# Transposes of q and x by TensorE in place of transposing transfers, in a linear-attention and MLP kernel

## The chip, the cores and the metric

The kernel runs on one core of one Trainium2 chip. The time is that of one execution on the device in microseconds (us), median of several runs. In the profile the engines are PE (TensorE, matmul) with PEld (its weight loads), DVE (VectorE), ACT (ScalarE), POOL (GpSimd) and SP (SyncE, which here only issues transfers).

## The reference

Eight batches of q, k and v go through linear attention with the feature map elu(x) + 1; the heads are joined to rows of 512, and these go through a two-layer MLP with the tanh form of GELU. Sizes: 8 batches, 8 heads, 576 positions, 64 per head; `w_in` 512 x 2048, `w_out` 2048 x 512.

```python
q_p, k_p = phi(q), phi(k)                       # phi(x) = where(x > 0, x, exp(x) - 1) + 1
kv = einsum('bhsd,bhse->bhde', k_p, v)
z = sum(k_p, axis=2)
num = einsum('bhsd,bhde->bhse', q_p, kv)
den = einsum('bhsd,bhd->bhs', q_p, z)[..., None] + 1e-06
x = (num / den) -> rows of 512 (heads joined), 4608 rows
h = x @ w_in
out = gelu_tanh(h) @ w_out
```

## The kernel before

**Tiling.** A batch has 576 positions. The first 512 are its main part, laid out as four chunks of 128 rows; the last 64 of all eight batches make one more part of 512 rows, the rest. Iterations j = 0 to 8 (`iteration`, L1065) each do the MLP of one part: 0 to 7 the main parts of the batches, 8 the rest. Iteration j also prepares the attention of the next part, and loads and maps for the ones after.

**The MLP of a part.** The hidden layer needs x with its 512 features on the partitions and the 512 rows along the free dimension: `xt`, four feature blocks of 128 x 512. Iterations 0 and 1 form h in sixteen blocks of 128 hidden features (`h_mm`, L354, words `p` in the orders; `g` is the GELU by ACT). From iteration 2 on half, and from 3 on all, of h comes in quads named X, Y, Z and W (`Quad`, L989): a two-by-two product in seven products in place of eight, each of four matmuls with 256 columns. Their operands are sums of quarters of `w_in` and of x; those of x are made by DVE in `sum_x` (L979, word `!xs`), four subtractions from the finished `xt`. Words of a quad are its products (X1 to X7), copies out of PSUM (s, m, u), additions (c, a) and GELUs (g11 to g22). The output layer has the same seven-product form (`Products.seeded`, L860, words `o1` to `o7`, each 16 matmuls with 256 columns; `S1` to `S4` are sums of hidden quarters by DVE, `os`, `ou`, `om`, `oc11` and so on are copies and additions of results).

**The attention of a part.** q, k and v are loaded by SP. The map is three instructions: the exponential by ACT (`!qe`, `!ke`), max(x + 1, 1) by DVE (`!qx`, `!kx`) and the smaller of the two by DVE (`!qm`, `!km`). v is cast by ACT or DVE (`!vc`). `kv_in_pair` (L629, word `k`) forms the key-value sums with 72 matmuls on 64-row tiles. `qt` is the mapped q with the feature dimension on the partitions; `nab` (L313, words `n0` to `n3`) multiplies a chunk of it with the key-value sums into a pair of PSUM banks (`nab_in_banks`, L319, into two single banks), and `divide` (L290) takes reciprocal and product on DVE and writes the chunk of x in rows, `xs`. The rest's q rows come in four tiles (`!rx`, `!re`, `!rm`).

**The transposes before.** In batches 0 and 1 q and x are transposed by TensorE: a matmul with an identity, 128 x 128 at a time into a PSUM tile `t_ps`, and a copy by ACT or DVE (`transpose_q`, L405 and L510; `transpose_x`, L346). For batches 2 to 7 and the rest, SP issues a transposing transfer from SBUF to SBUF for each chunk: `least_q` (L619) issues four for q as soon as the map is done, `least_rest` (L565) one for each rest tile, `transposed_x` (L641), called from `attention_piece` (L648), one for each chunk of x as soon as it is divided. They stand in SP's queue, in program order, between the loads.

**PSUM.** Of eight banks, six are single tiles (tag b): h blocks, quad products, output products, transposed blocks, and pieces in banks. Two form one pair, for attention pieces and key-value sums.

**What sets the order.** Nothing is scheduled at run time: each engine runs its instructions in the order in which the program issues them and waits on semaphores for its operands. That order is written out, one string of words for each iteration (ORDER_A to ORDER_I, L1123 on, for iterations 0 to 8). A prime after a word chooses the other engine for a copy, or for an `n` the two single banks. `@` runs work that is filed under a slot, among it stores; `!t` loads ACT's table for GELU.

Of the kernel before, what the change touches and what calls it, by code (L numbers as in the profile page):

```python
# [10 lines left out]
BF16 = mybir.dt.bfloat16  # L11
# [6 lines left out]
def kernel(  # L18
# [6 lines left out]
    moe_w_out: bass.AP,  # L25
    out: bass.AP,
):

    nc = tc.nc
# [5 lines left out]
    C = 4  # L41
# [40 lines left out]

    def pair_of_banks(name):
        return ps_a.tile([P, 2, 512], FP32, name=name, tag="a")

    ld = {}
# [90 lines left out]
    load_q(3)  # L179

    warm = pg.tile([P, 512], BF16, name="warm", tag="g")
    nc.vector.memset(warm, 0.0)
    ident = pth.tile([P, P], BF16, name="ident")
# [10 lines left out]

    def vp_paired(b):
        return vps[b % 2].rearrange("p (j u) e -> p j u e", u=NP)

    phi, exps, own = {}, {}, {}
# [37 lines left out]
    def least_of(name, b, hs=None, cs=None):  # L240
# [3 lines left out]
        if cs:  # L244
            p, e = p[:, cs], e[:, cs]
        nc.vector.tensor_tensor(p, p, e, op=ALU.min)

    def cast_v_paired(b, us, fn):  # L250
# [138 lines left out]
        nc.scalar.preload_act_table_set("gelu_apprx_tanh_and_others")  # L389

    BEGUN = (0, 1, 2, 3)

    def first_batch():
# [84 lines left out]
    first_batch()  # L480

    FIRST = 2
    fill = {}

# [77 lines left out]

    def least_rest(m):  # L565
        least_of("qr", m)
        if m == 0:
            qts[B] = pt.tile([P, C, NP, P], BF16, name="qt")
        nc.sync.dma_start_transpose(
            out=qts[B][:, m], in_=phi["qr", m][:, 0].rearrange("p h d -> p (h d)")  # L570
        )

    def cast_v_of(b, other):
        fn = nc.vector.tensor_copy if other else nc.scalar.copy
# [43 lines left out]

    def least_q(b, cs=slice(0, C)):  # L619
        least_of("q", b, cs=cs)  # L620
        if b not in qts:
            qts[b] = pt.tile([P, C, NP, P], BF16, name="qt")
        for c in range(cs.start, cs.stop):
            nc.sync.dma_start_transpose(
                out=qts[b][:, c],
                in_=phi["q", b][:, c].rearrange("p h d -> p (h d)"),
            )

    def kv_in_pair(b, fn=nc.vector.tensor_copy):  # L629
        kv_ps = pair_of_banks("kv_ps")  # L630
# [7 lines left out]
                in_=src[r],  # L638
            )

    def transposed_x(b, c, x):  # L641
        if b not in xts:
            xts[b] = pt.tile([P, NP, MAIN], FP16, name="xt")
        nc.sync.dma_start_transpose(out=xt_chunk(b, c), in_=x)

    x_parts = {}

    def attention_piece(b, c, in_banks=False):  # L648

        if b < B:  # L650
            return transposed_x(b, c, (nab_in_banks if in_banks else nab)(qts[b], b, c))
        if b not in x_parts:
            x_parts[b] = pxs.tile([P, C, d_model], FP16, name="xs")
        x = x_parts[b][:, c]
        if in_banks:
            n_ps = [bank("n_ps", [P, 4 * E]) for _ in range(2)]
        else:
            pair = pair_of_banks("n_ps")
            n_ps = [pair[:, s] for s in range(2)]
        bs = 2 * c, 2 * c + 1  # L660
        for i in range(2):
            for a in range(2):
                n = slice(E * (2 * i + a), E * (2 * i + a + 1))
                for t in range(2):
                    r = slice(HP * t, HP * (t + 1))
                    for s in range(2):
                        nc.tensor.matmul(
                            n_ps[s][r, n],
                            lhsT=qts[b][HP * s : HP * (s + 1), c, 2 * a + i, r],
                            rhs=kv_of_head(bs[t], s, 2 * a + i),  # L670
                            skip_group_check=True,
                        )
        x_v = x.rearrange("p (i s a d) -> p s i a d", s=2, a=2, d=D)
        if in_banks:
            for s in range(2):
                divide(x_v[:, s], n_ps[s].rearrange("p (i a e) -> p i a e", a=2, e=E))
        else:
            divide(x_v, pair[:, :, 0 : 4 * E].rearrange("p s (i a e) -> p s i a e", a=2, e=E))
        transposed_x(b, c, x)

    def evac(dst, src, on_scalar):
        (nc.scalar.copy if on_scalar else nc.vector.tensor_copy)(dst, src)
# [22 lines left out]
    def o_mm(o_ps, g, t, ms, half=None):  # L705
        for m in ms:
# [6 lines left out]
                start=(m == 0),  # L713
                stop=(m == MM - 1),
            )

    def w_out_sums():  # L720
# [344 lines left out]
    def iteration(j):  # L1065
# [10 lines left out]
        for word in ORDERS[j].split():  # L1076
# [26 lines left out]
                attention_piece(j + 1, int(name[0]), name.endswith("'"))  # L1103
            elif kind == "k":
                kv_in_pair(int(name))
            elif kind == "S":
                n, ms = name.split(":")
                products.sum(int(n), slice(*map(int, ms.split("-"))))
            elif kind == "T":
                products.third_sum(slice(*map(int, name.split("-"))), False)  # L1110
            elif kind == "!":
                what, _, b = name.rstrip("'").partition(":")
                if what == "vc":
                    cast_v_of(int(b), name.endswith("'"))
                elif b:
                    prepare_of[what](int(b))
                else:
                    prepare[what](j)
            else:
                name, other = name.rstrip("'"), name.endswith("'")  # L1120
                quads[kind].step(int(name) if name.isdigit() else name, other)
# [5 lines left out]
        "@32 o1:12-16 @33 !qe:2 o2:12-16 @34 o3:12-16 @35"  # L1127
    )
    ORDER_B = (
        "p0 !ke:2 p13 !lk:3 p1 !kx:2 !vc:2' !km:2 !t !qx:2 @2 p7 !qm:2 p2 g0 !bq !lv:3 !mq g1 g2 "  # L1130
        "p3 g3 k2 !a0 !a2 !a3 p6 p4 p5 p8 g4 p11 g5 !kxb:3 p9 g6 g7 T0-8 o1 os' g8 g9 p10 !qx:3 "
        "!kxa:3 g10 p12 o7 !lk:4 g11 p14 g12 g13 om S1:0-6 p15 S2:0-5 g14 g15 n1' o2 S1:6-8 "
        "S2:5-8 S4:0-6 n0 oc11' o6 !qe:3 n3' ou S4:6-8 !ke:3 n2 o5 oc22 !lq:4 !km:3 !vc:3 o4 oc21 "
        "o3 oc12' !qm:3 !ke:4 !xs !kx:4"
    )
    ORDER_C = (
        "!br k3 @1 Y1 Z1 !km:4 p6 Zs p0 !lk:5 !t g6 !lv:4 Z2 Zg11 Z6 p14 Z7 p8 Zu Z5 Zm g14 p7 g0 "
        "g8 Ys p15 !qx:4 Zc g7 Y6 Yu' Zg22 Y2 Yg11 Y7 Ym Z4 Za g15 n1 p1 g1 Y5 Yc Zg21 Y4 Ya Z3 "
        "Zg12 S1:4-8 n3 o1 Yg22 S2:4-8 p9 S1:0-1 S2:0-1 n2 Yg21 os g9 Y3 Yg12 S1:1-3 S1:3-4 "
        "S2:1-3 S2:3-4 S3:0-8 !qe:4 n0' o2 !lv:5 !qm:4 o6 oc11 ou o7 om o5 !kx:5 S4:0-8 oc22 "  # L1140
        "!ke:5 !vc:4 !xs o4 oc21 o3 !km:5 k4 oc12"
    )
    ORDER_D = (
        "!lq:5 !w0 Z1 X1 !t Y7 Y1 Xs X2 !w3 X7 @1 Ym' X6 Xg11 Ys n1 Xm' Y2 X4 Y6 Xu Xa X5 Yg11 Zs "
        "Xc Yu Xg21 n0 !lk:6 Y4 !vc:5' Z6 Zu X3 Xg12 Z2 Ya Y5 W1 Z7 Yc Zg11 Ws k5 Xg22 Zm Yg21 W6 "
        "Wu' Z5 Yg22 Y3 Yg12 !lv:6 Zc W7 Wm' W2 Z4 Za W5 Zg22 Z3 Wc W4 Wa n3 Wg11 Zg12 Zg21 o1 "
        "S1:0-6 Wg21 n2 os W3 Wg12 S2:0-6 !lq:6 Wg22 S1:6-8 S2:6-8 o2 !qe:5 S3:0-5 o6 S3:5-8 o7 "
        "S4:0-8 !qx:5 ou !qm:5 om !ke:6 oc11 o5 !lk:7 oc22 !vc:6 !kx:6 o4 o3 oc21 !xs oc12'"
    )
    ORDER_E = (  # L1150
        "X1 X7 Xm Xs Y7 !t X6 X2 Xg11 Xu' @1 Y1 Ym X4 X5 Ys Xa Xg21 Z1 Y2 Yg11 Zs !lr:0 Y4 Xc X3 "
        "!km:6 Y6 Yu n2 Z7 Xg12 Z6 Ya Z2 Zu Xg22 Yg21 n1 Zm W1 Z5 Y5 Yc Zc Zg11 Ws k6 Z4 Yg22 W7 "
        "Za Z3 Wm' Zg22 W6 Wu' n3 W4 Zg12 W2 Wg11 Wa Y3 W5 Wc Yg12 S1:0-6 S2:0-6 Zg21 Wg21 o1 os "
        "n0 Wg22 W3 Wg12 S1:6-8 S2:6-8 S3:0-8 !qx:6 o2 !lv:7 S4:0-8 !qe:6 o6 ou !lq:7 oc11 o7 om "
        "!xs o5 oc22 !re:0 o4 !re:1 !ke:7 !qm:6 oc21 !kx:7 o3 oc12'"
    )
    ORDER_F = (
        "!t !km:7 X1 Y1 Y7 !vc:7' Xs Ym' X6 X7 @1 X2 Xu Y4 Xm' !lr:1 X5 Xc X4 Xa Xg11 Ys k7 Y6 "
        "Yu' Y2 Xg22 Xg21 X3 Z1 Yg11 Zs !qx:7 Y5 W1 Yc Z2 Xg12 Ya Zg11 Z6 Zu Ws' Y3 Z7 Zm n1 Yg12 "
        "Z5 Yg22 W6 Wu S1:0-2 W7 Z4 W2 W5 Wm' Zc !rx:0 Zg22 Z3 Zg12 Wc Wg11 n0 Wg22 W4 S1:2-6 "  # L1160
        "S3:0-6 W3 Wg12 o1 os S1:6-8 S3:6-8 S2:0-8 n3 !qe:7 o7 om' o6 Wa Za Zg21 Yg21 ou' n2 o4 "
        "!qm:7 S4:0-6 o5 oc22 Wg21 o2 !rm:0 oc11 S4:6-8 o3 oc21 oc12 !xs"
    )
    ORDER_G = (
        "X1 n0 !rx:1 !rm:1 Xs Y7 Ym' X7 Xm' X2 X6 Xu' Xg11 Y1 Ys X4 Xa n2 X5 Y2 Z1 Xg21 Y6 Y4 "
        "Yg11 Zs W1 Xc Xg22 Yu' Ya !rx:2 X3 Xg12 Yg21 Y5 @1 Z6 Yc Z2 Z7 Zg11 Zu' Ws' Y3 Z5 Yg22 "
        "W7 Wm' W2 Wg11 Yg12 Zm Zc W6 Wu' W4 Zg22 Wa Z3 Zg12 Z4 W5 Za Zg21 Wc S1:0-6 o1 Wg21 "
        "S2:0-6 os n1 W3 Wg22 Wg12 S1:6-8 S2:6-8 S3:0-8 n3' o2 !rx:3 o6 o7 oc11' !re:2 ou S4:0-8 "
        "om o5 !re:3 !rm:2 oc22 o4 oc21 !rm:3 o3 !xs oc12' !t"
    )  # L1170
    ORDER_H = (
        "X1 Xs X7 Xm' n0' n1 X6 Xu X2 Xg11 X4 Y1 Xa X5 Y7 Xc Ys Y6 Xg21 Y2 Yg11 Yu' Z1 X3 W1 Zs "
        "Y5 Z6 Z2 Xg12 Ym Yc Y4 @1 Z7 Zu' Z5 Xg22 Zg11 Ya Y3 Ws W6 W2 Zm Yg21 Zc W7 Yg22 Wu' Wm "
        "Zg22 Wg11 Z3 Zg12 W5 Z4 Za Yg12 Zg21 Wc Wg22 W4 Wa S1:0-6 o1 os W3 Wg21 S2:0-6 Wg12 "
        "S1:6-8 S2:6-8 S3:0-8 n2 n3' o2 oc11 o6 ou o7 om o5 S4:0-8 o4 oc22 !xs o3 oc21 oc12'"
    )
    ORDER_I = (
        "X1 Y7 Ym X7 Xm Xs X2 Xg11 @1 X6 Y1 X4 Z1 Ys Y6 Xu' Xa Xg21 Y2 Y4 Yg11 Zs X5 Yu' Ya Y5 "
        "Yg21 Z7 Z2 Z6 W1 Xc Xg22 Zg11 Yc Y3 Yg22 Zu' X3 Ws' Z5 W6 Zm Zc Yg12 Wu W2 W7 W5 Wg11 Wm "
        "Zg22 Wc Xg12 Z4 Za Z3 Zg12 W4 Wa W3 Wg12 S1:0-6 S2:0-1 Wg22 o1 S1:6-8 S2:1-8 S3:0-8 o5 "  # L1180
        "Zg21 o6 Wg21 S4:0-8 o7 o2 o4 o3"
    )
    ORDERS = {0: ORDER_A, 1: ORDER_B, 2: ORDER_C, 3: ORDER_D, 4: ORDER_E, 5: ORDER_F, 6: ORDER_G, 7: ORDER_H, 8: ORDER_I}

# [33 lines left out]
```

## Time and profile before

| | |
|---|---|
| median of three runs | 265.94 us (265.37 to 266.69) |
| the profiled execution | 266.18 us |
| its span, first to last instruction | 264.4 us |
| first matmul of iterations 1, 2, 3, 4 | 48.30, 76.27, 104.15, 131.25 us |
| of iterations 5, 6, 7, 8 | 157.66, 184.31, 209.81, 235.33 us |
| end of the last matmul | 260.98 us |
| transposing transfers of x: number, median from issue to landing | 28, 2.3 us |
| of q | 24, 4.1 us |

The page of a profile gives the busy time of each engine over the span, then the span in 40 slices of 6.6 us, with a digit for the busy tenths, the granted clock of TensorE and the busy share of the 16 DMA engines. A view of windows gives the same for chosen stretches of time: length, then busy microseconds and number of instructions of each engine. A view of waits lists which engine sat idle before which tile and line, and what released it. The timeline lists instructions in order: start, duration, engine, line, operation, output and inputs, count. Matmuls overlap in the array, so the duration of a single one is longer than the distance to the next.

### The profile page before, as it was taken

The page shows a single profiled execution, that of the slowest core. Times are in us where ns is not written, and L with a number is a line of the kernel's source. Part 1 is how long each engine was busy: PE and PEld are TensorE (multiplying, and loading weights), DVE is VectorE, ACT ScalarE, POOL GpSimd, SP SyncE. Part 2 cuts the span into 40 slices and gives each one's busy share as a digit, 9 for nine tenths or more (in the row PEclk, how much of TensorE's full clock was granted, in tenths as well). Part 3 has the DMA queues.
Part 4 walks back from the last instruction along what each step waited for, and adds up shares of the span by engine and source line. Part 5 has one row for each costly group of instructions (what it writes and reads, how often), then busy time and mean ns, then how long its engine had stood idle before and what let it go on. Part 6 is the DMA issues. An engine that isn't in the chain of part 4 may idle for free. (4 is left out here: it accounts for less than half of the span.)

```text
span 264.4 us, 6675 instructions
## 1 busy us (share of the span) xinstructions
PE 257.3 (97%) x2765; PEld 203.0 (77%) x2765; DVE 227.7 (86%) x384; ACT 192.1 (73%) x279; POOL 18.8 (7%) x28
## 2 busy tenths in 40 slices
PE   8999999999999999999999999999999999989994
PEld 2584446446876788888888888989889888878883
DVE  3966497799989999999999999999999788868972
ACT  4768795955988788988898988884876478408810
POOL 8056501000000000000000000000000000000000
PEclk9999999999999999999999999999999999999999
DMA  6999999997969969999697398415620450112004
GB/s 235 402 405 397 409 409 396 407 304 217 222 152 286 327 112 222 346 261 241 191 264 195 57 347 236 82 40 68 174 102 21 126 134 2 24 57 121 2 0 159
DMA packets 59789, 53.90 MB, mean 204 GB/s; under 512 B 35696, under 2 KB 45936, under 8 KB 59760
## 3 DMA queue, kind: packets, MB, share of 16 engines
q1 hardware_dynamic: 56880, 44.57, 58.4%
q10 hardware_dynamic: 2880, 8.91, 9.4%
q8 instruction: 21, 0.34, 0.5%
q14 instruction: 8, 0.07, 0.1%
HBM read 36.70 MB, written 9.44 MB: 175 GB/s over the span
## 5 line engine op out<-in xcount | busy, mean ns | idle before, releaser
L784 PEld LDWEIGHTS <-g 128*128 128x128 f16 x624 | 60.5, 98 | 7.8 <-issue 0.4
L784 PE MATMUL o_ps<-w_out_sb,g 128*128 128x256 f16 x384 | 45.7, 273 | 0.0
L356 PE MATMUL h_ps<-xt,w_in_sb 128*128 128x512 f16 (+2 forms) x212 | 37.3, 327 | 0.0
L999 PEld LDWEIGHTS <-w_in_sb 128*128 128x128 f16 x312 | 30.1, 98 | 5.3 <-issue 1.5
L1014 ACT ACTIVATE g<-hq_ps 128x512 f16<-128x512 f32 x52 | 30.9, 622 | 3.9 <-DVE hq_ps L1027 2.5
L356 PEld LDWEIGHTS <-w_in_sb 128*128 128x128 f16 x212 | 18.0, 98 | 14.8
L784 PEld LDWEIGHTS <-s 128*128 128x128 f16 x272 | 26.5, 98 | 3.5
L376 ACT ACTIVATE g<-h_ps 128x512 f16<-128x512 f32 x40 | 22.2, 604 | 8.6 <-PE h_ps L356 8.3
L296 DVE TENSOR_TENSOR xs<-n_ps,r 128x512 f16<-128x512 f32 (+1 forms) x43 | 25.5, 592 | 1.5
L999 PEld LDWEIGHTS <-w_near 128*128 128x128 f16 x224 | 21.6, 98 | 3.5
L999 PE MATMUL hq_ps<-t_sum,w_near 128*128 128x256 f16 x168 | 24.1, 273 | 0.0
L1027 DVE TENSOR_TENSOR rows<-hq_ps,rows 128x512 f32<-128x512 f32 x26 | 17.6, 685 | 1.9 <-PE hq_ps L999 1.2
L1033 ACT COPY h_ps<-hq_ps 128x512 f32<-128x512 f32 x23 | 13.1, 571 | 8.2 <-PE hq_ps L999 7.7
L905 DVE TENSOR_TENSOR o_sb<-o_ps,o_sb 128x512 f32<-128x512 f32 (+1 forms) x21 | 13.3, 636 | 6.5 <-PE o_ps L784 3.6
L1027 DVE TENSOR_TENSOR hq_ps<-hq_ps,rows 128x512 f32<-128x512 f32 x26 | 17.8, 694 | 1.3 <-PE hq_ps L999 0.7
L230 ACT ACTIVATE k_e<-k_x 128x2304 bf16<-128x2304 f32 (+1 forms) x9 | 17.2, 1913 | 2.2 <-DVE o_sb L905 1.3
L1014 ACT ACTIVATE g<-rows 128x512 f16<-128x512 f32 x26 | 17.0, 652 | 2.4 <-DVE rows L1027 2.3
L1014 ACT ACTIVATE g<-h_ps 128x512 f16<-128x512 f32 x26 | 16.1, 621 | 3.2 <-PE h_ps L999 2.9
L230 ACT ACTIVATE q_e<-q_x 128x2048 bf16<-128x2048 f32 (+1 forms) x9 | 15.5, 1721 | 2.8 <-DMA q_x<-in_q_dram 2.8
L999 PE MATMUL h_ps<-xt,w_in_sb 128*128 128x256 f16 x104 | 15.6, 272 | 1.1 <-ACT h_ps L1033 1.0
L999 PE MATMUL hq_ps<-w_sum,w_in_sb 128*128 128x256 f16 x104 | 15.4, 272 | 0.0
L784 PE MATMUL o_ps<-w_sum,s 128*128 128x256 f16 x128 | 15.3, 273 | 0.0
(113 smaller groups left out, 456.2 us busy)
## 6 DMA issues: line engine op xcount, KB each, us to landing
out_dram<-o_sb ACTq DMA_DIRECT2D x16, 512.0 KB, 3.8
k_x<-in_k_dram SPq DMA_DIRECT2D x7, 1152.0 KB, 9.2
v_x<-in_v_dram SPq DMA_DIRECT2D x7, 1152.0 KB, 9.2
q_x<-in_q_dram SPq DMA_DIRECT2D x6, 1024.0 KB, 9.1
w_st<-in_moe_w_in_dram SPq DMA_DIRECT2D x3, 1024.0 KB, 13.4
q_x<-in_q_dram SPq DMA_DIRECT2D x4, 512.0 KB, 11.6
w_st<-in_moe_w_out_dram SPq DMA_DIRECT2D x2, 1024.0 KB, 12.6
w_st<-in_moe_w_out_dram SPq DMA_DIRECT2D x4, 512.0 KB, 11.1
```

What stands on the lines that cost most here:

```text
L230: nc.scalar.activation(o, i, AF.Exp)
L296: nc.vector.tensor_tensor(x_v, n_v[heads + (slice(0, D),)], r[heads + (None,)].to_broadcast(shape + [D]), op=ALU.mult,)
L356: nc.tensor.matmul(h_ps[:, ts], lhsT=w_in_sb[:, c, P * m : P * (m + 1)], rhs=xt[:, c, ts], start=(c == 0), stop=(c == KM - 1), skip_group_ ...
L376: nc.scalar.activation(g_v, h_v, AF.Gelu_apprx_tanh)
L784: nc.tensor.matmul(ps[t] if type(ps) is list else ps[:, t, :], lhsT=lhs[:, m, P * t : P * (t + 1)], rhs=rhs[:, m, :], start=(first and m = ...
L905: nc.vector.tensor_tensor(out, i0, i1, op=ALU.add)
L999: nc.tensor.matmul(ps[:, f], lhsT=lhs[:, c, P * f : P * (f + 1)], rhs=rhs[:, c], start=(first and f == 0 and c == 0), stop=(c == KM // 2 - 1),
L1014: nc.scalar.activation(g_v, src, AF.Gelu_apprx_tanh)
L1027: add = lambda out, i0, i1: nc.vector.tensor_tensor(out, i0, i1, op=ALU.add)
L1033: on(nc.scalar.copy, nc.vector.tensor_copy)(self.seed, self.b)
```

## The change

The transposing transfers of batches 2 to 7 and of the rest are gone. TensorE transposes instead, in halves of a part: two chunks of four blocks, so eight transposes into one single PSUM bank of 2-byte elements, and one copy of 1024 columns by ACT or, with a prime, DVE. New words place them in the orders: `!qta` and `!qtb` for the halves of q, `!rt` for a rest tile of four blocks, `t0` and `t1` for the halves of x (`t` in iteration j works on part j + 1). `attention_piece` only keeps the divided chunk. All orders but that of iteration 0 are written anew around these words, so that loads, maps, pieces and sums stand in other places, and some copies are on the other engine than before.

```diff
     def least_rest(m):
         least_of("qr", m)
-        if m == 0:
-            qts[B] = pt.tile([P, C, NP, P], BF16, name="qt")
-        nc.sync.dma_start_transpose(
-            out=qts[B][:, m], in_=phi["qr", m][:, 0].rearrange("p h d -> p (h d)")
-        )
...
     def least_q(b, cs=slice(0, C)):
         least_of("q", b, cs=cs)
-        if b not in qts:
-            qts[b] = pt.tile([P, C, NP, P], BF16, name="qt")
-        for c in range(cs.start, cs.stop):
-            nc.sync.dma_start_transpose(
-                out=qts[b][:, c],
-                in_=phi["q", b][:, c].rearrange("p h d -> p (h d)"),
-            )
...
-    def transposed_x(b, c, x):
+    def copied(other):
+        return nc.vector.tensor_copy if other else nc.scalar.copy
+
+    def transpose_q_half(b, s, other):
+        if b not in qts:
+            qts[b] = pt.tile([P, C, NP, P], BF16, name="qt")
+        t_ps = bank("t_ps", [P, 2, NP, P], BF16)
+        for c in range(2):
+            for i in range(NP):
+                nc.tensor.transpose(
+                    t_ps[:, c, i, :], phi["q", b][:, 2 * s + c, 2 * i : 2 * i + 2, :], ident
+                )
+        copied(other)(qts[b][:, 2 * s : 2 * s + 2], t_ps)
+
+    def transpose_rest(m, other):
+        if m == 0:
+            qts[B] = pt.tile([P, C, NP, P], BF16, name="qt")
+        t_ps = bank("t_ps", [P, NP, P], BF16)
+        for i in range(NP):
+            nc.tensor.transpose(t_ps[:, i, :], phi["qr", m][:, 0, 2 * i : 2 * i + 2, :], ident)
+        copied(other)(qts[B][:, m], t_ps)
+
+    def transpose_x_half(b, s, other):
         if b not in xts:
             xts[b] = pt.tile([P, NP, MAIN], FP16, name="xt")
-        nc.sync.dma_start_transpose(out=xt_chunk(b, c), in_=x)
-
+        t_ps = bank("t_ps", [P, NP, 2, P], FP16)
+        for c in range(2):
+            for i in range(NP):
+                x = chunks[b, 2 * s + c][:, P * i : P * (i + 1)]
+                nc.tensor.transpose(t_ps[:, i, c, :], x, ident_x)
+        copied(other)(
+            xts[b][:, :, 2 * P * s : 2 * P * (s + 1)], t_ps.rearrange("p i c n -> p i (c n)")
+        )
...
         if b < B:
-            return transposed_x(b, c, (nab_in_banks if in_banks else nab)(qts[b], b, c))
+            chunks[b, c] = (nab_in_banks if in_banks else nab)(qts[b], b, c)
+            return
...
-        transposed_x(b, c, x)
+        chunks[b, c] = x
...
     ORDER_B = (
-        "p0 !ke:2 p13 !lk:3 p1 !kx:2 !vc:2' !km:2 !t !qx:2 @2 p7 !qm:2 p2 g0 !bq !lv:3 !mq g1 g2 "
-        "p3 g3 k2 !a0 !a2 !a3 p6 p4 p5 p8 g4 p11 g5 !kxb:3 p9 g6 g7 T0-8 o1 os' g8 g9 p10 !qx:3 "
...
+        "p4 !ke:2 p0 !qx:2 p1 !bq !t p3 g0 !qm:2 !qtb:2' p2 p9 !a0 g1 g2 p5 g3 g4 !qta:2 @2 p12 "
+        "!kx:2 !a2 p6 g5 !mq !km:2 g6 p7 !vc:2' p8 !lk:3 g7 o1 p10 !qx:3 os g8 g9 g10 T0-8 !a3 "
...
     ORDER_E = (
-        "X1 X7 Xm Xs Y7 !t X6 X2 Xg11 Xu' @1 Y1 Ym X4 X5 Ys Xa Xg21 Z1 Y2 Yg11 Zs !lr:0 Y4 Xc X3 "
-        "!km:6 Y6 Yu n2 Z7 Xg12 Z6 Ya Z2 Zu Xg22 Yg21 n1 Zm W1 Z5 Y5 Yc Zc Zg11 Ws k6 Z4 Yg22 W7 "
-        "Za Z3 Wm' Zg22 W6 Wu' n3 W4 Zg12 W2 Wg11 Wa Y3 W5 Wc Yg12 S1:0-6 S2:0-6 Zg21 Wg21 o1 os "
-        "n0 Wg22 W3 Wg12 S1:6-8 S2:6-8 S3:0-8 !qx:6 o2 !lv:7 S4:0-8 !qe:6 o6 ou !lq:7 oc11 o7 om "
-        "!xs o5 oc22 !re:0 o4 !re:1 !ke:7 !qm:6 oc21 !kx:7 o3 oc12'"
+        "!kx:6 !qtb:5' X1 X7 Xm Xs Y7 !km:6 !t X6 Xu n2 X2 Xg11 Y1 Ys X4 Xa Z7 Ym' !lk:7 Xg21 X5 "
+        "Xc n1 Y2 !qx:6 Y6 Y4 Yu Ya @1 Z1 X3 Yg11 Zs Xg12 k6 Y5 Z2 Yc Z6 Zu' !lv:7 Yg21 Xg22 Zm "
+        "Zg11 W1 Ws' n3 W7 Yg22 Wm' Z5 Y3 Yg12 Zc Z4 Za W6 Wu W2 Wg11 Zg22 W4 Wa n0 W5 Z3 Zg12 Wc "
+        "Zg21 Wg21 S1:0-6 o1 Wg22 W3 Wg12 os' S2:0-6 S1:6-8 t1' S2:6-8 t0 S3:0-8 o2 !kx:7 o6 !xs "
+        "!qe:6 ou o7 oc11 om o5 S4:0-8 o4 !ke:7 oc22 !qm:6 !re:1 !re:0 o3 oc21 oc12 !km:7 !lq:7"
     )
...
```

## The prediction

> **What bounds the kernel now.** I read the page first (sums, slices), then the waits of TensorE, then the stretches of one iteration each, then the timeline for the price of a single matmul and a single transpose.
>
> ```profile
> span 264.4 us, 6675 instructions
> PE 257.3 (97%) x2765; PEld 203.0 (77%) x2765; DVE 227.7 (86%) x384; ACT 192.1 (73%) x279; POOL 18.8 (7%) x28
> ...
> PE   8999999999999999999999999999999999989994
> ...
> DVE  3966497799989999999999999999999788868972
> ...
> PEclk9999999999999999999999999999999999999999
> DMA  6999999997969969999697398415620450112004
> ```
>
> TensorE (PE) is busy in every slice, at the full clock; VectorE (DVE) is nearly as full from slice 9 to 30. "Busy" is not yet "at its peak", so I priced the work. In the timeline, 16 matmuls of 256 columns in a row last 1.91 us, and the last of them 0.27 us by itself, so one follows the other after (1.91 - 0.27) / 15 = 0.109 us. A row of 512 columns takes 0.216 us (below: 36.33 to 36.98 for three).
>
> ```profile
> 150.67 1.91 PE L784 MATMUL o_ps<-w_out_sb,g 128*128 128x256 f16 x16
> ```
> ```profile
> 48.30:76.27 27.97, 27.40 (x263) 18.27 (x260) 25.71 (x38) 20.64 (x26) 0.00 (x0) 1.00 0.84 253
> ...
> 104.15:131.25 27.10, 26.76 (x320) 23.43 (x313) 26.36 (x46) 24.38 (x36) 0.00 (x0) 1.00 1.00 246
> 131.25:157.66 26.41, 26.37 (x315) 23.32 (x313) 25.66 (x42) 22.51 (x35) 0.00 (x0) 1.00 0.77 218
> 157.66:184.31 26.65, 26.59 (x314) 23.25 (x312) 25.85 (x44) 20.18 (x31) 0.00 (x0) 1.00 0.54 116
> ```
>
> These stretches are iterations 1 and 3 to 5 (length first, then busy PE, weight loads, DVE, ACT, POOL, clock, DMA share, GB/s). Iteration 4 issues 28 quad products of 4 matmuls and 7 output products of 16: 224 x 0.109 = 24.4 us; 16 attention matmuls at 0.057 (0.9); one group of 72 small key-value matmuls (0.7). That is 26.1 of its 26.4 us. Done so for all of iterations 1 to 8, the work is 26.8 + 27.6 + 26.1 + 26.1 + 26.1 + 25.3 + 25.3 + 24.4 = 207.7 us, and the stretch from 48.30 to TensorE's last matmul at 260.98 is 212.7. So at most 5.0 us in 213 are not matmul issue. The waits of PE inside that stretch agree; no transfer is among them:
>
> ```profile
> PE h_ps L999 <- ACT h_ps L1033: 1.0, 2, 0.8
> PE kv_ps L262 <- DVE k_p L246: 0.5, 1, 0.5
> ```
>
> The kernel is bound by how many columns TensorE streams, with DVE a close second.
>
> **TensorE's part of the change.** Blocks that move to it: q of batches 2 to 7, 6 x 16 = 96; x of batches 2 to 7 and of the rest iteration, 7 x 16 = 112; the rest rows' q, 4 x 4 = 16. In all 224 transposes with as many weight loads. Batch 1 already does this, and the trace shows the price:
>
> ```profile
> 36.33 0.81 PE L709 MATMUL o_ps<-w_out_sb,g 128*128 128x512 f16 x3
> 36.98 1.06 PE L516 MATMUL t_ps<-ident,q_p 128*128 128x128 bf16 x16
> 37.87 0.81 PE L709 MATMUL o_ps<-w_out_sb,g 128*128 128x512 f16 x3
> ```
>
> Sixteen transposes hold the engine from 36.98 to 37.87, 0.89 / 16 = 0.0556 us each; the lone 0.219 us is latency that the next one overlaps. 224 x 0.0556 = 12.5 us. Nothing in TensorE's list is removed for it: the matmuls of the products, attention pieces and key-value sums are the same number and shapes. By iteration (1 to 7) the blocks are 48, 32, 24, 24, 32, 40, 24, or 2.7, 1.8, 1.3, 1.3, 1.8, 2.2, 1.3 us; iterations 0 and 8 get none. Since TensorE has no room, this lies on the path.
>
> The skill has two prices here. "TensorE: Matmul & The Clock Gate", section Back-to-back issue gap, gives about 81 ns for each 128-column matmul in a stream with weight loads; by it the 224 cost 18.1 us, where this trace has 56 ns. "VectorE: DVE Perf Modes", section The three transpose paths, sets 390 ns on TensorE against 1309 ns by transfer, and its rules table prefers TensorE; read as cost that speaks for the change, but the trace shows the transfers taking none of the bound engine's time.
>
> **Entering and leaving a group.** There are 30 groups (12 of q, 14 of x, 4 of rest rows). Lower bound 0: the group above starts 0.65 us after three 512-column matmuls began, which is just their 3 x 0.216. Upper bound: the small key-value matmuls, with 64-row tiles, lose about 0.1 us on the way in and 0.1 on the way out, so 30 x 0.2 = 6 us. I take 0, from the row of the same operation, and keep 6 for the range.
>
> **The copies out of PSUM.** By the built order ACT takes 13 copies of eight blocks and one of four, DVE 13 and three.
>
> ```profile
> L521 ACT COPY qt<-t_ps 128x1024 bf16<-128x1024 bf16 x2 | 1.9, 1015 | 0.3 <-PE t_ps L516 0.3
> ...
> L744 DVE TENSOR_TENSOR s<-g 128x1024 f16<-128x1024 f16 x2 | 1.4, 686 | 0.2 <-ACT g L1014 0.2
> ...
> L350 DVE COPY xt<-t_ps 128x512 f16<-128x512 f16 x2 | 0.8, 425 | 0.4 <-PE t_ps L349 0.4
> ```
>
> ACT: 13 x 1.015 + 0.59 = 13.8 us, and one more table load (1.28). DVE: 13 x 0.69 + 3 x 0.43 = 10.3 us, where the 1024-wide copy is an estimate from the 1024-wide subtraction, nearest in size and type; bounds are 0.425 (half as wide) and 1.015 (ACT's). The new order also moves six seed copies and some other evacuations between ACT and DVE, and sends five attention pieces fewer through two single banks (2 x 0.60 us on DVE) and more through the pair (0.89), saving 1.5. Counting every word of both orders at its row's mean, DVE's list grows by 10.4 us and ACT's by 12 and the table load. Over iterations 1 to 5 DVE was busy 130.7 of 136.0 us; it gets 7.3 more while TensorE gets 160 x 0.0556 = 8.9: 138.0 of 144.9, no fuller than before. Between iterations 3 and 5 it is tighter: 77.9 of 80.2 becomes 83.5 of 84.6, since key maps move into iteration 4. If DVE packs there no better than the present 97%, those three last 86.0 and lose 1.4. ACT stays far below, hidden beside TensorE. Lower bound of this term 0, upper some 3 (twice the computed loss); I take 1.
>
> **The transfers.** SP's queue loses 56 transposes, each of which stood there waiting for DVE (up to 14.5 us) with loads behind it. The loads come earlier; nobody waited: of DVE's waits after 48.3, 1.4 us were for x's transpose and 1.0 for a load, and the weight loads lost 0.2 to q's. If TensorE waits only as it did, the gain is 0; the upper bound is all 5.0 us of slack. I take 0, because the waits above have other releasers. In place of the transfer's 2.3 us (x) and 4.1 us (q) until landing, x now goes DVE divide, TensorE, copy, DVE sums. What is queued behind a transpose that comes before its divide is done is all of TensorE; the orders put one to two output products (1.74 us each) between a piece and its transposes, which covers reciprocal and multiply, 0.84 us, as long as DVE is not behind. The first products of the next iteration wait for the copy and the first difference, 1.0 + 0.4 us; one output product (1.74) and often a q half stand between.
>
> **PSUM.** A transposed half holds one of six single banks for about a microsecond, where it held none. At the start of iteration 1 four h blocks, the half and a fifth block fill six; the next block then waits for the first gelu, by some 0.2 us. Inside the 1 us above.
>
> **Sum.** The profiled execution took 266.18 us (span 264.4), the median of three is 265.94, so 0.24 comes off: 266.2 + 12.5 + 1.0 - 0.2 = 279.5.
>
> **Rivals.**
> 1. *DVE, ACT or PSUM become the bound*, and TensorE stalls at transposes and next to them. For it: DVE's 99% in iterations 3 to 5, three steps instead of one transfer before each next x, 30 groups with entries. Against it: cumulative DVE share falls. Price, over 266.0 + 12.5 = 278.5: 4.5 us where half of both upper bounds (3 and 6) comes true, 9 where all does: 283 to 287.5. It decides when the time after 48.3 us that is not matmul issue, now 5.0, passes 9.5.
> 2. *TensorE's slack pays part.* For it: SP's queue is freed and DVE's waits for transfers, 2.6 us, go. Against: TensorE itself hardly waits. All 5.0 us recovered gives 273.9, half 276.4.
> 3. *Not slower: transfers slow the chip's SBUF traffic, and without them matmuls and vector work run faster.* DMA engines are 98 to 100% busy in iterations 2 and 3. To break even every matmul of the 212.7 us must go 5.9% faster, 0.109 to 0.103. Against it: in iteration 8, at DMA share 0.16, a stretch of x16 lasts the same 1.91 us as at 150.67, and the clock is full already. Worked out: no change in matmul price, so 0 gain; it would have to be wholly hidden from this profile. If it were so, 265 or less.
> 4. *The change does not do what it says.* The built SP list holds no transposes any more and TensorE 448 more rows: excluded.
>
> **How the numbers follow.** Chances: the forecast case (276.5 to 283) 0.75; rival 1 beyond that 0.17; rival 2 below 276.5 0.06; rival 3 0.02. The likeliest gives 279.5. Low 276.5 leaves out half of the slack's recovery and better; high 284.5 takes in 266.2 - 0.2 + 12.5 with the entry bound of 6, and the lower part of rival 1. About 0.5% (1.3 us) can be told from no change here. Faster 0.02 (rival 3), same 0.01, slower 0.97: even with all the slack gone the sum stands 8 us above the time before.
>
> **What would show it.** TensorE: 2989 matmuls, transposes 0.056 apart; iteration 4 about 27.8 us and iteration 1 about 30.5 to 31 us; the start until 48.3 and the 3.4 us after the last matmul unchanged. DVE busy near 237, ACT near 205. DMA share lower throughout. Wrong if transposes are spaced 0.08 or more, if new waits of PE on DVE or ACT sum above 4 us, or if 256-column matmuls change from 0.109.

## The result, and the profile after

The changed kernel takes 277.91 us (median, 277.54 to 278.34) against 266.06: 1.0447 times as long, 95% interval 1.0416 to 1.0477. The prediction was 279.5 with a range from 276.5 to 284.5.

The page of the changed kernel, its profiled execution (278.34 us):

```profile
span 276.5 us, 7000 instructions
PE 269.6 (98%) x2988; PEld 215.0 (78%) x2989; DVE 235.2 (85%) x390; ACT 204.6 (74%) x291; POOL 17.4 (6%) x28
...
PE   8899999999999999999999999999999999999995
...
DVE  3983487898999999999999999997999879856982
...
DMA  6999999996475249550691074000300021012004
```

TensorE is still full, and the DMA engines, mostly busy until slice 25 before, are now idle for long stretches. The same iterations as before, 1 and 3 to 5, in the view of windows (length, then busy PE, weight loads, DVE, ACT, POOL, clock, DMA share, GB/s):

```profile
49.05:79.08 30.03, 29.83 (x311) 20.90 (x309) 27.55 (x38) 24.19 (x30) 0.00 (x0) 1.00 0.75 268
...
108.70:137.03 28.33, 27.99 (x339) 24.57 (x337) 27.43 (x46) 25.27 (x34) 0.00 (x0) 1.00 0.44 129
137.03:164.57 27.54, 27.54 (x339) 24.77 (x336) 26.99 (x43) 23.68 (x35) 0.00 (x0) 1.00 0.49 167
164.57:193.42 28.85, 28.52 (x347) 24.99 (x345) 25.74 (x43) 22.02 (x32) 0.00 (x0) 1.00 0.16 52
```

Iteration 4 grew from 26.41 to 27.54 us, 1.13; its 24 transposes account for 1.33, so 0.2 us that was not matmul issue has gone from it. In the timeline a group of eight stands between quad products as if it had always been there: it ends and the next product starts 0.45 us after the group began.

```profile
165.01 0.60 PE L1010 MATMUL hq_ps<-xt,w_in_sb 128*128 128x256 f16 x4
165.44 0.61 PE L627 MATMUL t_ps<-ident,q_p 128*128 128x128 bf16 x8
165.89 0.38 PE L1010 MATMUL hq_ps<-t_sum,w_more 128*128 128x256 f16 x2
```

The whole difference of the spans, 276.5 - 264.4 = 12.1 us, comes out on TensorE:

| term | us |
|---|---|
| 224 transposes, mean distance inside a group 0.0559 | +12.5 |
| not matmul issue between the start of iteration 1 and the last matmul: 5.0 before; after, 273.12 - 49.05 = 224.1 less 207.7 + 12.5 = 220.2 of work, 3.9 | -1.1 |
| iteration 1 starts at 49.05, before at 48.30 (see the last section: it happens with either program) | +0.75 |
| after the last matmul: 3.4 both times | 0 |

The waits of PE between 48.3 and 273 us show no transpose either, and are fewer than before:

```profile
PE hq_ps L1010 <- DVE rows L1053: 0.3, 1, 0.3
PE h_ps L347 <- ACT g L367: 0.2, 1, 0.2
```

So far the forecast and its working hold: 224 more matmuls, 27.54 us for iteration 4 (forecast 27.8), DVE busy for 235.2 us (237) and ACT for 204.6 (205). Iteration 1 took 30.03 us, a little under the 30.5 to 31 forecast, and did not start at 48.3. Whether TensorE's columns are the cause, and whether one could get the 12 us back by taking parts away, is another question, and there the runs gave surprises.

### The profile page after: what moved, and what is told of

Same layout as the page of the kernel before. It is cut to its first block, busy times and chain, and to the rows that moved or that the text cites. A ratio compares the mean times of both kernels' runs of the same rounds, so it can differ in the third digit from the quotient of the medians.

```text
span 276.5 us, 7000 instructions
## 1 busy us (share of the span) xinstructions
PE 269.6 (98%) x2988; PEld 215.0 (78%) x2989; DVE 235.2 (85%) x390; ACT 204.6 (74%) x291; POOL 17.4 (6%) x28
## 5 line engine op out<-in xcount | busy, mean ns | idle before, releaser
L347 PE MATMUL h_ps<-xt,w_in_sb 128*128 128x512 f16 (+2 forms) x212 | 37.9, 327 | 0.2 <-ACT g L367 0.2
L287 DVE TENSOR_TENSOR xs<-n_ps,r 128x512 f16<-128x512 f32 (+1 forms) x38 | 24.7, 649 | 1.3
L1044 ACT COPY h_ps<-hq_ps 128x512 f32<-128x512 f32 x19 | 10.9, 572 | 7.4 <-PE hq_ps L1010 7.1
L795 PE MATMUL o_ps<-w_near,s 128*128 128x256 f16 x128 | 15.3, 273 | 0.0
```

The lines of the kernel that those rows point to most:

```text
L287: nc.vector.tensor_tensor(x_v, n_v[heads + (slice(0, D),)], r[heads + (None,)].to_broadcast(shape + [D]), op=ALU.mult,)
L347: nc.tensor.matmul(h_ps[:, ts], lhsT=w_in_sb[:, c, P * m : P * (m + 1)], rhs=xt[:, c, ts], start=(c == 0), stop=(c == KM - 1), skip_group_ ...
L795: nc.tensor.matmul(ps[t] if type(ps) is list else ps[:, t, :], lhsT=lhs[:, m, P * t : P * (t + 1)], rhs=rhs[:, m, :], start=(first and m = ...
L1044: on(nc.scalar.copy, nc.vector.tensor_copy)(self.seed, self.b)
```

## The experiments

In the expectations theory 1 is that of the prediction (TensorE's columns cost, nothing else), theory 2 its first rival (copies by ACT and DVE, and waits for them), theory 3 its third (without transfers all else runs faster), theory 4 that the new order by itself costs or gains, theory 5 a mixture. Beside the experiments the kernel before took 265.54, 265.96 and 266.44 us (medians of three sets), so differences of less than about 1 us between runs of different sets are not read.

**More of TensorE's work, less of the copies.** First, every transpose twice, copies as they are:

```diff
             for i in range(NP):
-                nc.tensor.transpose(t_ps[:, i, c, :], x, ident_x)
+                for _ in range(2):
+                    nc.tensor.transpose(t_ps[:, i, c, :], x, ident_x)
```

> Every transpose is issued twice into the same place, all else as in the changed kernel. Theory 1 (the change costs the columns that TensorE streams, 0.0556 us for each of 224 blocks, and nothing else): 277.9 + 12.5 = 290.4 us, within 1.5. Theory 2 (the copies by ACT and DVE, or the waits for them, are a good part of the 11.9 us; TensorE has room beside them): the second transpose is partly hidden, 284 or less.

Measured: 289.02 us, 11.1 more than the changed kernel. That is inside theory 1's 290.4 within 1.5, at its lower edge, and theory 2's 284 is out. Of the spans, 287.2 against 276.5, the difference is 10.7: 12.5 for the second transposes, less 0.7 (this execution began iteration 1 at 48.36) and 1.2 of idle time used up (235.4 us from there to the last matmul, less 220.2 and 12.5, leave 2.7 in place of 3.9). Second, all transposes but copies of one block alone:

```diff
-        copied(other)(qts[b][:, 2 * s : 2 * s + 2], t_ps)
+        copied(other)(qts[b][:, 2 * s, 0], t_ps[:, 0, 0])
...
-        copied(other)(
-            xts[b][:, :, 2 * P * s : 2 * P * (s + 1)], t_ps.rearrange("p i c n -> p i (c n)")
-        )
+        copied(other)(xts[b][:, 0, 2 * P * s : 2 * P * s + P], t_ps[:, 0, 0])
```

> The changed kernel with all its transposes, but each copy takes only one of the eight (or four) blocks out of PSUM, into fixed tiles that alternate by batch; the rest of q and x keeps older values, so that part of the computation is left out. Of 24 us of copies some 8 are left. Theory 1 (columns of TensorE set the time, the copies are hidden): 276 to 278 us. Theory 2 (the copies are the larger part of the 11.9 us): 272 or less. Theory 5 (TensorE's columns and the copies each demand nearly the whole 11.9 by themselves, since TensorE and the pair of DVE and ACT were both full, so that taking away one alone gives little): 274.5 to 277.5, and with both taken away the time falls to that of the kernel before.

Measured: 277.97 us. The copies' rows show what was taken away; of the changed kernel, then of this one (busy us, mean ns):

```profile
L648 ACT COPY xt<-t_ps 128x1024 f16<-128x1024 f16 x8 | 8.0, 1013 | 0.3 <-PE t_ps L647 0.3
...
L630 DVE COPY qt<-t_ps 128x1024 bf16<-128x1024 bf16 x7 | 4.7, 686 | 0.9 <-PE t_ps L627 0.8
```
```profile
L651 ACT COPY xt<-t_ps 128x128 f16<-128x128 f16 x8 | 2.0, 264 | 0.3 <-PE t_ps L650 0.3
...
L633 DVE COPY qt<-t_ps 128x128 bf16<-128x128 bf16 x7 | 1.5, 221 | 1.2 <-PE t_ps L630 1.1
```

ACT was busy for 195.1 in place of 204.6 us and DVE for 229.9 in place of 235.2, and the time is the same (1.0443 times the kernel before, against 1.0447). In the changed kernel what was taken away, some 17 of 24 us of copies, was hidden entirely. Theory 1 stands, and theory 2's 272 is out; theory 5's 277.5 is passed by too little to count, and its second half is the next experiment.

**Less of TensorE's work.** One transpose for each group, the copy reading it eight times (first run); and one transpose with a copy of that block alone (second run):

```diff
-        for c in range(2):
-            for i in range(NP):
-                x = chunks[b, 2 * s + c][:, P * i : P * (i + 1)]
-                nc.tensor.transpose(t_ps[:, i, c, :], x, ident_x)
-        copied(other)(
-            xts[b][:, :, 2 * P * s : 2 * P * (s + 1)], t_ps.rearrange("p i c n -> p i (c n)")
-        )
+        nc.tensor.transpose(t_ps[:, 0, 0, :], chunks[b, 2 * s][:, 0:P], ident_x)
+        for_all = t_ps[:, 0, 0:1, :].to_broadcast([P, 2 * NP, P])
+        to = xts[b][:, :, 2 * P * s : 2 * P * (s + 1)].rearrange("p i (c n) -> p i c n", c=2)
+        copied(other)(to, for_all.rearrange("p (i c) n -> p i c n", c=2))
```

> One transpose in place of eight (or four) per group; the copy keeps its size and engine and reads that one block eight times, so q and x are not transposed rightly and this part of the computation is left out. Theory 1: 194 blocks fewer, 277.9 - 194 x 0.0556 = 267.1 us, within 1. Theory 2 (copies and waits cost): above 271. Theory 3 (without transfers on the chip all else runs faster, the change's hidden gain): below 265.5, since only 30 blocks (1.7 us) remain of TensorE's extra work.

```diff
-        copied(other)(to, for_all.rearrange("p (i c) n -> p i c n", c=2))
+        copied(other)(xts[b][:, 0, 2 * P * s : 2 * P * s + P], t_ps[:, 0, 0])
```

> One transpose in place of eight (or four) and a copy of that one block alone, into the fixed tiles; the rest of q and x keeps older values. Theory 5: TensorE is relieved of 10.8 us, DVE and ACT of 16, and no transfer is left to wait for: 265 to 268 us. If the new order by itself costs (theory 4): 271 or more.

Measured: 275.02 and 273.55 us. Both miss theory 1: 10.8 us of TensorE's work were gone and only 2.9 came back; with the copies gone as well, 4.4. The first lies where theory 2 was expected (above 271), but without the copies the second is only 1.5 lower, and it misses theory 5's 265 to 268. Of the second run's span (271.3, 6.9 above the kernel before) 1.7 are the 30 blocks left. Gaps of more than 0.2 us beyond the usual distance between matmuls that follow each other, after iteration 1 began, sum to 7.3 us there, against 3.4 in the kernel before and 1.7 in the changed one with small copies. They lie at fifteen places, none above 0.91; seven of them, 4.1 us in all, stand directly behind a transposed group, which now holds TensorE for 0.056 us in place of up to 0.45. The longest waits of PE in that run:

```profile
PE o_ps L788 <- DVE o_sb L909: 1.3, 2, 0.7
PE hq_ps L1003 <- DVE rows L1046: 0.9, 2, 0.5
PE h_ps L788 <- DVE h_ps L878: 0.8, 2, 0.5
PE t_ps L635 <- DVE qt L629: 0.6, 1, 0.6
```

The first three are results of the products themselves, and only the fourth is of a transposed block's copy. The reading that fits is that the written order of the changed kernel gives DVE and ACT just the time that TensorE's longer list leaves: shorten TensorE's list and it runs into them. So theory 4 holds in this form: the new order is some 5 us worse than the old one for a kernel with hardly any transposes. That it would be so with none at all was not run. Theory 3 falls here too: these two runs have no transposing transfer and hardly any transpose, and are slower than the kernel before, with 256-column matmuls 0.109 us apart in all of them.

**The old transfers in the new order.**

```diff
+        for c in range(C):
+            nc.sync.dma_start_transpose(
+                out=qts[b][:, c], in_=phi["q", b][:, c].rearrange("p h d -> p (h d)"),
+            )
...
-        "qta": lambda b, other: transpose_q_half(b, 0, other),
+        "qta": lambda b, other: None,
...
-            chunks[b, c] = (nab_in_banks if in_banks else nab)(qts[b], b, c)
-            return
+            return transposed_x(b, c, (nab_in_banks if in_banks else nab)(qts[b], b, c))
```

> The new orders with the old transfers, issued as before as soon as a map or a chunk is done; no transposes by TensorE and no copies. Theory 1: 277.9 - 12.5 = 265.4 us, equal to the kernel before within 1, so the order is neutral. Theory 4 (the new order is by itself better or worse than the old one, and the cost of the transposes is accordingly more or less than 11.9): under 264.4 or over 267.5.

Measured: 282.36 us, slower than the changed kernel though TensorE and both copying engines are relieved. The longest wait of PE is 3.4 us before an attention piece in iteration 5, for the cast `kvbd`. That cast stands in DVE's list behind the map of a q whose load landed late:

```profile
172.84 0.70 DVE L1053 TENSOR_TENSOR hq_ps<-hq_ps,rows 128x512 f32<-128x512 f32 x1 [0.61 <-PE hq_ps L1025]
177.44 1.23 DVE L230 TENSOR_SCALAR q_p<-q_x 128x2048 bf16<-128x2048 f32 x1 [3.90 <-DMA q_x<-in_q_dram]
178.59 0.86 DVE L624 CAST kvbd<-kv_ps 64x260 bf16<-64x260 f32 x2
```

That load was issued at 171.16 us, after four transposes of q that held SP from 165.23 to 171.06; in the changed kernel the same load went out at 158.55:

```profile
165.23 5.83 SPq L612 DMA_TRANSPOSE qt<-q_p  x4
171.16 0.53 SPq L99 DMA_DIRECT2D q_x<-in_q_dram  x1
```

My theory then was that the loads' place behind waiting transposes made this run slow. The test gave the loads to another queue (those of q and of the rest rows likewise):

```diff
-        nc.sync.dma_start(out=ld[name, b][:, us, :], in_=s[:, us, :])
+        (nc.sync if b < 3 else nc.gpsimd).dma_start(out=ld[name, b][:, us, :], in_=s[:, us, :])
```

> The new orders with the old transfers (as in the run with 282.4 us), but the loads of q, k and v that are issued in the iterations, and the rest rows, go from POOL's queue, so that none of them stands behind a transfer that waits. If the loads' place behind the transfers made that run slow: 10 or more of its 17 us over theory 1 go, 268 to 273. If the latency of the transfers themselves does it: 279 or more.

Measured: 295.5 us in one run and 306.8 in the other; either is past the 279 expected if the latency of the transfers themselves is the cause. The wait behind the late load is gone from PE's list, but another, 11.3 us, has come. It is the one that now leads, here with the transposes of q in the list of transfers, the last number the median us from issue to landing:

```profile
PE n_ps L269 <- DMA qt<-q_p: 11.3, 5, 4.6
```
```profile
qt<-q_p SPq DMA_TRANSPOSE x24, 7.1
```

Beside loads from a second queue a transpose of q took 7.1 us, where it took 3.5 with all in one queue and 4.1 in the kernel before. So the run traded one cost for a larger one, and does not show what the loads' place was worth by itself. In both runs PE waits for transposing transfers; in the kernel before, with the old orders, none is among the releasers of its waits. How the 17 us by which the old transfers in the new order missed theory 1 split between late loads, late transposes and the 5 us of the new order itself stays open.

Half of the change each, in the new orders. With x by TensorE, q and the rest rows are transferred:

```diff
-        "qta": lambda b, other: transpose_q_half(b, 0, other),
-        "qtb": lambda b, other: transpose_q_half(b, 1, other),
-        "rt": transpose_rest,
+        "qta": lambda b, other: None,
+        "qtb": lambda b, other: None,
+        "rt": lambda m, other: None,
```

> New orders; x by TensorE (112 blocks), q and the rest rows' q by transfers as before. Theory 1: 277.9 - 112 x 0.0556 = 271.7 us within 1. If the waits of x's half, copy and sums at the start of the next iteration cost: more than 273.

With q by TensorE, x is transferred:

```diff
             elif kind == "t":
-                transpose_x_half(j + 1, int(name[0]), name.endswith("'"))
+                pass
```

> New orders; q and the rest rows' q by TensorE (112 blocks), x by transfers as before. Theory 1: 271.7 us within 1, and the savings of this and of the kernel with x by TensorE add up to 12.5. If q's part is hidden or is the dearer one: off by 2 or more, with the other off the other way.

Measured: 279.98 us with only x by TensorE and 280.21 with only q, each 2 to 3 slower than with both, where theory 1 had 271.7. It is the same finding from another side. TensorE's time that is not matmul issue is 12.3 us in both, in place of 3.9, and the columns saved are 6.3. With x by TensorE, PE's longest wait, 2.4 us, leads by the same `kvbd` to the same late load of q; with q by TensorE, the longest, 2.3, is for a transfer of x. How much of the rest comes from TensorE's shorter list alone, as in the runs with small copies, is not separated.

**The old order with transposes by TensorE.** The transposes stand where the transfers were issued, with their copies on ACT and DVE in turn:

```diff
     def transposed_x(b, c, x):
         if b not in xts:
             xts[b] = pt.tile([P, NP, MAIN], FP16, name="xt")
-        nc.sync.dma_start_transpose(out=xt_chunk(b, c), in_=x)
+        chunks[b, c] = x
+        s = c // 2
+        if (b, 2 * s) in chunks and (b, 2 * s + 1) in chunks:
+            t_ps = bank("t_ps", [P, NP, 2, P], FP16)
+            for c in range(2):
+                for i in range(NP):
+                    x = chunks[b, 2 * s + c][:, P * i : P * (i + 1)]
+                    nc.tensor.transpose(t_ps[:, i, c, :], x, ident_x)
+            (nc.scalar.copy, nc.vector.tensor_copy)[s](
+                xts[b][:, :, 2 * P * s : 2 * P * (s + 1)], t_ps.rearrange("p i c n -> p i (c n)")
+            )
```

> The kernel before with its old orders, the transposes by TensorE where the transfers were issued: right after the map, and after the second chunk of a half; ACT and DVE take turns at the copies. If the new order does nothing but place words: 266.1 + 12.5 = 278.6 us. If the placing hides the wait for the divide (reciprocal and multiply 0.84 us, plus DVE's backlog of 1 to 2 us) and the copy: 30 groups x 0.5 to 1.5 us more on TensorE, 290 to 315.

Measured: 335.89 us, 58 more than the changed kernel with as many instructions on TensorE; I had at most 315. The waits of PE and the granted clock in 40 slices:

```profile
PE t_ps L655 <- DVE xs L296: 25.8, 16, 3.9
PE t_ps L628 <- DVE q_p L246: 8.8, 5, 4.7
PE t_ps L571 <- DVE rows L246: 2.9, 2, 1.8
```
```profile
PEclk9999998797779969999999999999996999869999
```

TensorE stood for up to 4.7 us before a group, 37.5 us in these three lines, and the clock, full in the changed kernel, fell in nine slices of 8.4 us (mean 0.944). Behind several of the waits the matmuls were slower too. Here a group waits for 3.89 us, and the output product after it lasts 3.40 us where it lasts 1.91 at the full clock; the view of windows has a granted clock of 0.50 there:

```profile
119.59 1.04 PE L655 MATMUL t_ps<-ident_x,xs 128*128 128x128 f16 x8 [3.89 <-DVE xs L296]
120.41 3.40 PE L800 MATMUL h_ps<-w_out_sb,g 128*128 128x256 f16 x16
```
```profile
116.60:123.40 6.80, 3.81 (x22) 2.95 (x23) 3.99 (x9) 3.72 (x3) 0.00 (x0) 0.50 0.42 132
```

**The copies on one engine.**

```diff
     def copied(other):
-        return nc.vector.tensor_copy if other else nc.scalar.copy
+        return nc.scalar.copy
```

> All 30 copies of transposed blocks on ACT; ACT gets 13 x 1.0 + 3 x 0.6 = 15 us more (204.6 to some 219 of 276), DVE 9 to 10 less. Theory 1 (only TensorE's columns count): 277.9 within 1.5. Theory 2 (DVE is the second bound and its copies cost): below 276. If ACT's latency (1.0 us against 0.6 to 0.7) or its backlog comes before the next matmul: 280 or more.

```diff
     def copied(other):
-        return nc.vector.tensor_copy if other else nc.scalar.copy
+        return nc.vector.tensor_copy
```

> All 30 copies on DVE: 13 x 0.6 to 0.7 + 0.4 = 9 us more on DVE, ACT 13.8 less. Theory 1: 277.9 within 1.5. Theory 2 (DVE is full in iterations 3 to 5, so what is added there comes out at the end): 4 to 9 us more, 282 to 287.

Measured: 290.54 us with all on ACT, 285.5 with all on DVE, so 12.6 and 7.6 more; the second is inside theory 2's 282 to 287, the first past the 280 expected where copies come late. Of the three splits they are hidden only with the one that the order writes. The waits of PE with all on ACT name the results that came late:

```profile
PE o_ps L795 <- ACT o_sb L894: 3.2, 2, 2.8
PE hq_ps L1010 <- ACT h_ps L1044: 3.1, 2, 2.7
PE h_ps L1010 <- ACT h_ps L1044: 1.9, 1, 1.9
```

The longest of them, 2.8 us, is before a product that waits for a copy (`o_sb`) which ACT began only at 75.87 us. Before that, ACT had stood idle for 3.88 us until the transposes of a half of x were done, and then copied it (1.01), loaded a table (1.28) and formed an exponential (1.91). So the place of the copies in ACT's list costs here, and not their duration alone.

**A mend of the kernel before.** The prediction's list of waits named two places that are worth half a microsecond or more. One block of iteration 1 goes ahead of the key-value sums that wait, and one store of iteration 7 goes to SP, since ACT's next copy waited behind it:

```diff
-        "p3 g3 k2 !a0 !a2 !a3 p6 p4 p5 p8 g4 p11 g5 !kxb:3 p9 g6 g7 T0-8 o1 os' g8 g9 p10 !qx:3 "
+        "p3 g3 p6 k2 !a0 !a2 !a3 p4 p5 p8 g4 p11 g5 !kxb:3 p9 g6 g7 T0-8 o1 os' g8 g9 p10 !qx:3 "
...
-            nc.scalar.dma_start(out=ov[:, 2 * h : 2 * h + 2], in_=o_sb)
+            (nc.sync if j == B - 1 else nc.scalar).dma_start(out=ov[:, 2 * h : 2 * h + 2], in_=o_sb)
```

> The kernel before with two small mends at TensorE's longest waits: in iteration 1 the block p6 goes ahead of the key-value sums that wait for the map of k (0.7 us), and in iteration 7 the second store is issued by SP and not by ACT, whose seed copy waits behind it (0.9 us). If these waits are on the path: 264.4 to 265.3 us against 266.0. If something else ends the wait: 266.0.

Measured: 265.56 us against 266.44 for the kernel before beside it, 0.9 less where 0.7 to 1.6 were expected; the ratio is 0.998 (0.9964 to 0.9996), so the gain is small and barely clear of none. Both waits are gone: no PE wait is left in the view after 48 us, and gaps above 0.2 us sum to 1.5 in place of 3.4. From the start of iteration 1 to the last matmul this execution took 211.3 us in place of 212.7.

## Why the prediction was right, and where it was not

- *TensorE's columns.* 224 x 0.0556 = 12.5 us: measured 0.0559 apart, at the full clock. The row from batch 1 was the right price, and doubling the transposes put 11.1 on top once more. The Trainium skill's 81 ns for a 128-column matmul in a stream with weight loads ("TensorE: Matmul & The Clock Gate", Back-to-back issue gap) would have put an estimated 18.1 us on a change that cost 11.9; the trace does not agree with it.
- *Entering and leaving a group.* Taken as 0, right: where a 256-column matmul precedes a group, its distance to the first transpose is 0.109 us, and the distance out is 0.056 except at two places (0.27 and 0.36, waits).
- *Copies.* The term was mis-sized: 1 us, from DVE in iterations 3 to 5, measured 0 (277.97 with one block of each copy). I had computed 83.5 us of DVE work for 84.6; busy there were 27.43 + 26.99 + 25.74 = 80.2 of 84.7. The durations of single instructions overlap on DVE, as its timeline in the changed kernel shows (0.69 us long, the next one 0.60 after it started), and adding them counts the overlap:

```profile
141.26 0.69 DVE L1038 TENSOR_TENSOR hq_ps<-hq_ps,rows 128x512 f32<-128x512 f32 x1
141.86 0.68 DVE L1038 TENSOR_TENSOR rows<-hq_ps,rows 128x512 f32<-128x512 f32 x1
```

  That the copies are hidden is true of the written split only, as the runs on one engine show.
- *Transfers.* "The gain is 0" was 1.1 us off: TensorE's time without matmul issue fell from 5.0 to 3.9. The two longest gaps of before, 0.9 and 0.7 us, are not there after; in the mended kernel before they go by two moves in the order, with all transfers in place. So the order is the likelier cause, but the runs do not separate it from the missing transfers.
- *The sum.* 279.5 against 277.9. For the profiled execution the forecast is 0.2 more, 279.7, against 278.34: 1.3 too much, which is the two terms above, 1.0 and 1.1, less the 0.75 of the late start, which the profile of before did not have. That the late start took back over a third of the two errors is luck.
- *Rivals.* The first (DVE, ACT or PSUM as the bound) did not come true, but lies close: it is what happened in the runs that touched the split of the copies or the order. The second came true in size by not quite a quarter, 1.1 of 5.0 us, its cause open. The third is out. Two sums of the working are off, and nothing hangs on them: 24.4 + 0.9 + 0.7 is 26.0 and not 26.1, and from 278.5 the second rival's prices are 273.5 and 276.0, not 273.9 and 276.4.
- What the prediction did not see: that the price is not had back by removing parts of what was added. I treated the new orders as a list of places. By the runs they are part of the change: the old order with the new operation costs 70 us, the new order with the old operation 16.4. A lower bound for any order with the same start and end, an estimate from the profile alone, is 48.3 + 220.2 of work + 3.4 = 271.9 us of span, 7.5 above the 264.4 of before.

## What to carry to other kernels

Where one engine streams without gaps, price moved work by its distance in the trace, not by its duration, and put all of it on the path; work on engines beside it costs nothing as long as the order was written with it in place. In a kernel with a fixed order on each engine, an operation and the order around it can't be judged apart: undoing or halving the operation in the new order measures the order as well. When a wait is to be removed, look first at what the engines do in order just before it: moving one word and one store removed the two longest ones here.

## What the runs showed of the hardware that was not expected

**Two starts.** Iteration 1 begins at 48.2 to 48.4 us in seven of the fourteen profiles and at 49.0 to 49.1 in the other seven, with kernels built from either program. The first map instruction on DVE differs; of the kernel before and the changed one, each with POOL's memsets at that time:

```profile
4.57 0.94 DVE L238 TENSOR_SCALAR q_p<-q_x 128x1024 bf16<-128x1024 f32 x1 [3.44 <-DMA q_x<-in_q_dram]
```
```profile
3.49 2.97 POOL L195 MEMSET kvbd<- 128x520 bf16 x5
```
```profile
4.77 1.70 DVE L230 TENSOR_SCALAR q_p<-q_x 128x1024 bf16<-128x1024 f32 x1 [3.64 <-DMA q_x<-in_q_dram]
```
```profile
3.50 2.43 POOL L188 MEMSET kvbd<- 128x520 bf16 x5
```

In every profile with the early start one memset lasts 1.07 us instead of 0.53 or 0.54 and DVE's instruction 0.93 to 1.11; in every one with the late start all memsets beside it keep that length and DVE's instruction 1.3 to 2.0. So in each profile one of the two engines was slowed, and never both. That was seen side by side; why it is so was not tested, nor was a kernel tried with the memsets at another time.

**The clock.** It was 0.944 in mean where TensorE stood 37.5 us in all before its transposes, and 1.0 in the changed kernel. In the old order it stood at 0.5 in stretches of 3.4 or 6.8 us beside some of the longer waits, and 256-column matmuls were 0.21 us apart there in place of 0.109. Not every long wait did it: the one of 3.4 us in the new order with the old transfers left the clock at 1.0. What decides it these runs do not show.

**Transposing transfers beside loads.** In the new orders a transpose of q took 3.5 us from issue to landing with the loads in its queue, and 7.1 with the loads in POOL's (medians of 24).
